# A new order table for the steps of an attention, token-mixer and routed-attention kernel

## The chip, the cores and the metric

The kernel runs on 1 core of a Trainium2 chip. The metric is the device time of one execution in microseconds (us), the median of several runs; lower is better. One core has five engines with an instruction queue each: TensorE (PE in the rows; PEld is its weight load), VectorE (DVE), ScalarE (ACT), GpSimd (POOL) and SyncE (SP), which here only issues transfers between DRAM and the on-chip memory. Each engine takes its own list strictly in order; an instruction that waits for another engine or for a transfer holds everything behind it on its own engine.

## The reference

Three stages, one after the other, for 4 batches of 448 tokens. A first attention has 12 heads of width 64 on normed queries and keys; a mixer works over tokens (448 to 256 and back) and over channels (768 to 1536 and back); a second, causal attention has 4 experts of width 64, of which each token uses two.

```python
def _attn_ref(q, k, v, g_q, g_k):
    q_n, k_n = (rmsnorm(q, g_q), rmsnorm(k, g_k))
    scores = scale * np.matmul(q_n, k_n.transpose(0, 1, 3, 2))
    scores = scores - np.max(scores, axis=-1, keepdims=True)
    attn = np.exp(scores)
    attn = attn / (np.sum(attn, axis=-1, keepdims=True) + 1e-09)
    return np.matmul(attn, v)
def _moe_ref(x, w_tok1, w_tok2, w_ch1, w_ch2):
    h = np.maximum(x.transpose(0, 2, 1) @ w_tok1, 0.0) @ w_tok2
    u = x + h.transpose(0, 2, 1)
    return u + np.maximum(u @ w_ch1, 0.0) @ w_ch2
def _moe2_ref(x, w_gate, wq, wk, wv, wo):
    # two largest gate logits of each token, softmax over these two: w
    for e in range(E):
        q, k, v = x @ wq[e], x @ wk[e], x @ wv[e]
        scores = np.where(causal, -1e9, scale * (q @ k.transpose(0, 2, 1)))
        a = softmax(scores)
        out += w[token, e] * (a @ v @ wo[e])
```

## The kernel before

The whole computation is cut into 3,840 steps. A step is a few instructions on one engine: the scores of one or two chunks of 112 queries (`weighted`, line 712 on PE), the row maxima (line 682 on DVE, written to `nm`), their scaling (line 688, on DVE or POOL), the exponentials (line 697 on ACT, out of the accumulator banks `s` into the tiles `s`), the flips of the weights (PE transposes, line 736, into the banks `a`, each then copied out by `copy` on ACT, line 541, or on DVE, line 542), the product with the values (`attend`, line 835), the transposes of its result (line 861), and the large products with the weights (`product`, line 630). The accumulator banks `s`, `m` and `a` are rings of two buffers: the third user waits until the first has been copied out.

For batch 0 the first attention comes by itself; from then on the side work (the first attention of batch b+1 and the second of batch b-1) stands among the products of `channel(b)`, whose weights are loaded into the ring `whl` of 6 buffers, the first time from the inputs, later from copies in DRAM (`kept_c1`, `kept_c2`, line 621).

For the pairs of heads of batches 1 to 3 `spread` (lines 773 to 799) turns the sums of the exponentials into a row: two small DVE operations on `inv` (lines 782 and 784), a write of the row to DRAM (line 786), and two reads of it, spread over the partitions, into `rn` (line 798). In `normalize` the reciprocal `rc` (line 869) stands ahead of the scaling of the transposed result into `xn` (line 880). In `project` the gate is some 30 small DVE operations (`tiny`).

The order of the steps is not found when the kernel is built. `Plan.issue` reads it from a table, a compressed string in which each step has its place and its engine:

```python
def issue(self):
    ...
    for k in self.read():
        self.steps[k][2](self.by[k])
```

The costs that steps are added with, and their `port` mark (this step and the steps of the other engine with that mark don't run together), are used by `lay` and `order`, a model that lays steps out in time; `issue` calls neither.

Of the kernel before, what the change touches and what calls it, by code (L numbers as in the profile page):

```python
# [21 lines left out]
EPS_SUM = 1e-9  # L22
# [34 lines left out]
    r"c-nPY3w#vSxu5@;nIyXl2_zv2gg3||SV0sE3Mk%dTPjk4i&e3p0yY&yt@MI`dVeVRs#IIAC~rj+sD%pD=jEXwjr9Q{Mo=NVl"  # L57
    r"Mo<4LfB+?=iKkSW@h8Pi@TYfbI$ktfB)~B)nY)(W$<jEF^4sccs~vsx4Nt2cc2cbEM%e{iAYlp>U!Zg-oW$|0OPFf0-S&QZ0"
    r"lPxf0he+vBKoMSR-aU|Jok3-!$hd^u0FIeP{K+_X<w6ImL=9Sph#qyYkTPn2kp<x69OV%w0J9Sr>KL_cQ)%W0t#d*doMFvd;"
    r"Wa!F`KyR0!prjuqkO__}1o!N2eax*pDKyJ5sM9G?@L)2VbOJ2?2>$Dc_3#li2JGMmUux5K6_+%2kzp6HK*rwiKMnd#2%SI$m"  # L60
    r"caiRz(OBb@@<QG>uSr<^rcySr#?#IVuHZWw(1AlHiq+_BnR=@FAXY!U7j&|Q*EOmDBis3u1M(!q9d4p<;vANeL(s6p{k!`z1"
    r"@weL#aOYowv0L4buL92Bn322ed~fH{gBO1o`xZLZ58htf?I2K}o9JFK(A{+4#YcO8da0ZFb!IUe=<c*(7m~E0-@bJJi=~)y{"
    r"fPnRHeOP?_=<yN1KMB8xLx$>&nRYgHAB&f$VYr6B?U+<M{dibli0gB{PUHAzuPgg?YFr&HJPnDoqww9`hLZ408h82!}O1#1t"
    r"@_IeI_zqMaM^m?Xd4&$_L+%O|`k_++?)w&eZe;k<IwUW79`>x#ioh3f+Qne8J;Q5f535rjSFMH;oy(wJ`H&GWOD)8Hr&wFJJ"
    r"mRrravCP4CwxT=~xz{;+JxKM`3taoI<^ZO$LL1@`ear;3~Yo;R(0u-J$p==ptlpKWL@zm0fm%wKQKYmHj=#<*6%x=FRI9vmt"
    r"bYW6-xcXP3xLc5lYMelt>QtNvUboW)Qo7yI|el(#k8+q<Y+ImSDP*p9?pbhe**jZ~aW?c(RJ(9f|wJqV)c0Iek=ojp4YvlGV"
    r"pZ|}gI~T0OXl&+`K;)lRhq_?jCQN9PLxFndCi>_@dEIh=%>0iEH@7U`KACUFxQirq=G((gAcu}@1ai^S-Z8qSoW5Oc@95S#&"
    r";6)3kHq--6ml<kJePl0-S1e>ok9<K?H3l-^lHHlbp>nbZX0tT&T6}V(VyXb6RQ<Q<YiMV_xE7z80*Q|XBcoOUe%vgIs)59xg"
    r"WR5$M*JMefhcV9WF<0xfCm2RfEv_pS_Wvx2$Iy6ktzLS=SRo`8%1MUG<rL9nS9?h_XRga~Y(=`DK(eO8OU7-K$s$@O9BO>#w"
    r"G&-8S0Ymy5R<A41zs7NR3xIg#(}jpxUIIPSUWo7)Wiq_$^)UA4aum#mzM+4GT6Q!UkR9Jz6tjN{o9@;)87+5V9DV>~Ss;3T?"  # L70
    r"UwWfOe-<DqM_Iv+yZp9@v3;q*m36@ir{n>K<^1TZy$c372oIP-H{%oX{aCZMM$F^AXLFM0C;^A4JUq8Xda`%IRYwLIaYeezF"
    r"Q8$0Y?`ic^*--o*6ANmj|3XQ@eN;O~TJZdN*s++c96zgf3;Sp9#U3pk_iov*%AVqjN-L=rVr0_1TONwL(e)EojEC1__A?Lfe"
    r"F5|SZA&~do4;<4i#^ig+^NF4kz4rWWix>3k$42Ky;wsG58({qWWmMX)-Rt#Fi3t_$x(m*np@XC@cM6_Xc3Q!IMij=%~*MHRD"
    r"C@zt7^Mw((<!+FaE_&J8~9Nm;R2HmrQ=?VeiT@XYx_K;E$!(QH(aNaDKB2tLf^tEW{&m&?mB%zPl=Gd>n4-E!5rd)~|2a47M"
    r"t(5rWeikypHdPu~5>RE&D16fc*2^-aYGBzh}`*$W=9J^LB#y$t18at~X~c&aq%3cET3PRgOeKhS#aG=lnvH@tNv(Cy7nr~QR"
    r"3cyN(Tv;g<FOC}TK3nyV{$C8sjX?5<A1~;qz*b8+0ucFKZ-L(4SIb4Mec^EnLUy(O{`84nnro35)dyraF@8YgSrJUJpdHuco"
# [353 lines left out]
def kernel(  # L430
# [20 lines left out]
    S = CP * NCH  # L451
# [966 lines left out]
```

## Time and profile before

| what | us |
|---|---|
| median of 3 runs | 835.11 |
| lowest and highest run | 835.08, 835.37 |
| the profiled execution, its own time | 836.71 |
| span of its instructions | 834.6 |
| TensorE busy in the span | 809.7 |
| VectorE, ScalarE, GpSimd busy | 614.1, 478.8, 128.7 |

The span goes from the first to the last instruction of the profiled execution; the 2.1 us to its own time lie around it. The granted clock of TensorE is at its upper level in nearly all of the span.

### The profile page before, as it was taken

The numbers are of one execution on the slowest core, as the hardware profiler recorded it, in microseconds if no ns is written. First come the engines' busy times: TensorE is split into PE (matmuls) and PEld (weight loads), VectorE is DVE, ScalarE is ACT, GpSimd is POOL, SyncE is SP. The second block draws the span as 40 slices with busy tenths as digits, with TensorE's granted clock in tenths as the row PEclk, the third lists the DMA queues.
The fourth block names the chain that finished last, engine by engine and source line by source line (L and its number), as shares of the span: only waits on it lengthen the run. The fifth ranks groups of instructions, "written<-read, shape, count | busy, mean of one in ns | idle before, by whom it ended". The sixth has DMA issues, their size and how long they took to land.

```text
span 834.6 us, 13125 instructions
## 1 busy us (share of the span) xinstructions
PE 809.7 (97%) x4508; PEld 631.6 (76%) x4508; DVE 614.1 (74%) x1298; ACT 478.8 (57%) x1053; POOL 128.7 (15%) x154
## 2 busy tenths in 40 slices
PE   4999899999999999999999999999999999999998
PEld 1446597878667878778776977767877888999886
DVE  6999999989999896977888688786665665221362
ACT  6898886777889548465466447643653631011243
POOL 3024201121542014130011010101120020000100
PEclk9999999999999999999999999999999999999999
DMA  8658879989876467887647515784666306776444
GB/s 227 179 176 202 261 238 272 303 284 287 277 241 194 146 191 250 236 286 219 207 139 207 204 29 172 237 230 163 207 194 176 126 2 207 211 219 201 150 145 174
DMA packets 83202, 168.37 MB, mean 202 GB/s; under 512 B 17504, under 2 KB 39136, under 8 KB 83136
## 3 DMA queue, kind: packets, MB, share of 16 engines
q1 hardware_dynamic: 82992, 167.54, 65.9%
q8 instruction: 36, 0.59, 0.3%
q14 instruction: 30, 0.25, 0.1%
q10 hardware_dynamic: 144, 0.00, 0.0%
HBM read 136.66 MB, written 30.84 MB: 201 GB/s over the span
## 4 chain that ended last, share of the span: by engine, by line
PE 87%; DMA 4%; DVE 4%; ACT 3%; issue 1%; SPq 0%; ACTq 0%; DVEq 0%
PE a L630 61%; PE s L712 10%; PE m L835 10%; PE m L861 2%; PE s L760 2%; ACT s L697 1%; DMA nat<-in_nat_dram 1%; PE a L736 1%; DMA whl<-kept_c 1%; PE s L736 1%; DMA xhl<-in_nat_dram 1%; DVE nm L682 1%; DMA rn<-inv 1%; ACT s L541 0%; DVE st L938 0%
## 5 line engine op out<-in xcount | busy, mean ns | idle before, releaser
L630 PE MATMUL a<-uhl,whl 128*128 128x448 f32 x1152 | 240.7, 364 | 0.1
L630 PEld LDWEIGHTS a<-uhl,whl 128*128 128x128 f32 x1152 | 213.7, 188 | 24.6 <-issue 6.8
L630 PE MATMUL a<-hid,whl 128*128 128x448 f32 x864 | 180.2, 365 | 1.7 <-DMA whl<-kept_c 1.6
L630 PEld LDWEIGHTS a<-hid,whl 128*128 128x128 f32 x864 | 160.3, 187 | 23.7 <-issue 8.5
L697 ACT ACTIVATE s<-s,nm,st 128x448 f32<-128x448 f32 (+1 forms) x192 | 137.5, 723 | 57.6 <-DVE nm L688 41.1
L822 ACT COPY s<-s 32x896 f32<-32x896 f32 (+1 forms) x134 | 111.1, 829 | 39.6 <-DVE s L810 37.9
L712 PE MATMUL s<-k,q 64*128 64x448 f32 (+4 forms) x512 | 111.3, 549 | 4.8 <-ACT s L697 4.1
L682 DVE TENSOR_REDUCE nm<-s 128x2 f32<-128x896 f32 (+1 forms) x96 | 101.6, 1079 | 11.7 <-PE s L712 11.5
L835 PE MATMUL m<-s,v 128*64 128x448 f32 x384 | 77.5, 545 | 0.7 <-ACT s L822 0.7
L712 PEld LDWEIGHTS s<-k,q 64*112 64x112 f32 (+1 forms) x512 | 41.3, 184 | 48.3 <-issue 26.3
L1219 DVE TENSOR_TENSOR u<-a,u 128x448 f32<-128x448 f32 x48 | 29.8, 621 | 57.6 <-PE a L630 57.5
L810 DVE STREAM_TRANSPOSE s<-s 128x896 f32<-128x896 f32 x60 | 63.5, 1088 | 4.1 <-ACT s L697 2.7
L822 DVE COPY s<-s 32x896 f32<-32x896 f32 (+1 forms) x91 | 59.1, 650 | 2.3
L835 PEld LDWEIGHTS m<-s,v 128*64 128x64 f32 x384 | 25.8, 136 | 43.2 <-issue 39.6
L697 ACT ACTIVATE s<-s,nm 112x448 f32<-112x448 f32 (+3 forms) x64 | 31.0, 493 | 38.0 <-DVE nm L676 37.4
L546 ACT ACTIVATE hid<-a 128x448 fp32r<-128x448 f32 x27 | 14.6, 541 | 66.1 <-PE a L630 65.9
L1208 DVE SCALAR_TENSOR_TENSOR hid<-a,hid 128x448 fp32r<-128x448 f32 x48 | 29.6, 619 | 30.8 <-ACT hid L546 30.3
L560 POOL TENSOR_TENSOR uhl<-u,uhl 128x448 fp32r<-128x448 f32 x23 | 27.7, 1219 | 148.8 <-DVE uhl L542 141.7
L560 POOL TENSOR_TENSOR whl<-wraw,whl 128x384 fp32r<-128x384 f32 (+1 forms) x28 | 29.8, 1067 | 110.4 <-ACT whl L541 43.5
L630 PE MATMUL a<-whl,uhl 128*112 128x260 f32 x288 | 38.6, 287 | 0.0
L697 ACT ACTIVATION_READ_ACCUMULATOR s<-s,nm,st 128x1 f32 (+1 forms) x192 | 38.3, 199 | 0.0
L676 DVE CUSTOM_DVE_ANT_0 s<-s,veil 112x112 f32<-112x112 f32 (+3 forms) x64 | 28.3, 461 | 12.5 <-PE s L712 11.5
(149 smaller groups left out, 1039.3 us busy)
## 6 DMA issues: line engine op xcount, KB each, us to landing
whl<-kept_c SPq DMA_DIRECT2D x144, 384.0 KB, 4.0
w<-in_wc_dram SPq DMA_DIRECT2D x48, 384.0 KB, 3.9
kept_c<-whl SPq DMA_DIRECT2D x48, 384.0 KB, 4.7
whl<-kept_qk SPq DMA_DIRECT2D x24, 384.0 KB, 3.7
nat<-in_nat_dram SPq DMA_DIRECT2D x19, 448.0 KB, 5.2
v<-in_vals_dram SPq DMA_DIRECT2D x24, 256.0 KB, 6.5
q<-in_qkt_dram SPq DMA_DIRECT2D x24, 232.0 KB, 5.6
k<-in_qkt_dram SPq DMA_DIRECT2D x22, 224.0 KB, 4.9
```

The costliest lines, as they stand in the source:

```text
L560: either(n, reads, writes, lambda e: e.tensor_tensor(dst()[:, 1], src(), f(dst()[:, 0]), op=ALU.subtract))
L630: nc.tensor.matmul(acc, lhs[:, x], rhs[:, y], start=first and i == 0, stop=last and i == 2)
L676: dve(w + 40, [], [pst, (nm, (c, j))], lambda e, j=j: e.tensor_tensor_reduce(pst.t[:CP, j, :w], pst.t[:CP, j, :w], veil[:, S - w :], -1.0, ...
L682: lambda e: e.tensor_reduce(nm.t[:R, c], pst.t[:R, :, :w], axis=AX.X, op=ALU.max, negate=True))
L697: lambda j=j: nc.scalar.activation(s.t[:, c, j, :w], pst.t[:R, j, :w], AF.Exp, bias=nm.t[:R, c, j : j + 1], scale=-1.0 if rq is None else ...
L712: nc.tensor.matmul(pst.t[:R, j, :w], q.t[me, CP * c : CP * c + R], k.t[me, :w], start=True, stop=True)
L736: nc.tensor.transpose(ps()[:, i, CP * r : CP * r + CP], s.t[:, r].rearrange("p j k -> p (j k)")[:, P * m : P * m + P], ident[:CP, :CP])
L810: dve(2 * S - 4, [(s, (j, r)) for j in range(2)], [(t, r)], lambda e, r=r: e.transpose(t.t[:, :, 32 * r : 32 * r + 32], s.t[:, r].rearrang ...
L822: lambda e, a=a, o=o, w=w, at=at: (nc.scalar.copy if e == "ACT" else ENG[e].tensor_copy)(at(p.t[32 * o : 32 * o + 32, :, P * a : P * a + N ...
L835: nc.tensor.matmul(av.t[64 * j : 64 * j + 64, q0:S], vat(j, c)[1](), p.t[:, j, c, q0:] if causal else p.t[:, 3 * j + c], start=c == 0, sto ...
L1208: lambda e, hl=hl, pa=pa: e.scalar_tensor_tensor(hl.t[:, 1], pa.t[:, :S], 0.0, f(hl.t[:, 0]), op0=ALU.max, op1=ALU.subtract))
L1219: dve(S, [pa], [u], lambda e, u=u, pa=pa: e.tensor_add(u.t, pa.t[:, :S], u.t))
```

## The change

The table is another one. The same 3,840 steps with the same dependencies are issued in another order, and 381 of them on another engine (of those that can run on two or three): GpSimd has 133 steps instead of 122, VectorE 1,140 instead of 1,153, ScalarE 798 instead of 796, TensorE (1,202) and SyncE (567) as many as before. Of TensorE's steps 797 stand at another place of its list. Two groups of small VectorE steps get the `port` mark, which only the model reads. The longer table moves all later line numbers up by 8: line 736 before is line 744 after.

```diff
 TABLE = (
-    r"c-nPY3w#vSxu5@;nIyXl2_zv2gg3||SV0sE3Mk%dTPjk4i&e3p0yY&yt@MI`dVeVRs#IIAC~rj+sD%pD=jEXwjr9Q{Mo=NVl"
...
         mine = lambda: inv.t[:CP, : 2 * NCH]
         dve(2 * NCH, [p.sm], [inv], lambda e: e.tensor_scalar_add(
-            mine(), p.sm.t[:CP].rearrange("p j c -> p (j c)"), EPS_SUM))
-        dve(80, [], [inv], lambda e: e.reciprocal(mine(), mine()))
+            mine(), p.sm.t[:CP].rearrange("p j c -> p (j c)"), EPS_SUM), port=True)
+        dve(80, [], [inv], lambda e: e.reciprocal(mine(), mine()), port=True)
...
-        tiny = lambda reads, writes, fn: add("DVE", 78, reads, writes, fn)
+        tiny = lambda reads, writes, fn: add("DVE", 78, reads, writes, fn, port=True)
```

**VectorE at the end of the first attention of batch 0.** Before, in front of the scaling of the last result (`xn`, in the trace at 100.5 us); `m_1085` and `m_1136` are the transposed results of two head pairs:

```order
L868 TENSOR_SCALAR rc_1124<-sm_669 112x16
L580 SCALAR_TENSOR_TENSOR wraw_1106<-wraw_1106,w_1000 128x384
L542 CAST whl_1127<-wraw_966 128x384
L582 SCALAR_TENSOR_TENSOR wraw_1106<-w_1000,wraw_1106 128x384
L542 CAST whl_1130<-wraw_966 128x384
L930 SCALAR_TENSOR_TENSOR k_898<-k_898,gqk,rb_991 128x448
L560 TENSOR_TENSOR whl_1130<-wraw_966,whl_1130 128x384
L560 TENSOR_TENSOR uhl_1025<-u_851,uhl_1025 128x448
L560 TENSOR_TENSOR whl_1127<-wraw_966,whl_1127 128x384
L869 RECIPROCAL rc_1124<-rc_1124 112x16
L880 TENSOR_TENSOR xn_1144<-m_1085,rc_1124 112x4x128
```

After, the same place (`m_1116` and `m_1140` are the two transposed results):

```order
L876 TENSOR_SCALAR rc_1084<-sm_676 112x16
L550 CAST whl_1086<-wraw_950 128x384
L877 RECIPROCAL rc_1084<-rc_1084 112x16
L588 SCALAR_TENSOR_TENSOR wraw_1079<-wraw_1079,w_989 128x384
L590 SCALAR_TENSOR_TENSOR wraw_1079<-w_989,wraw_1079 128x384
L550 COPY oT_1121<-m_1088 128x448
L888 TENSOR_TENSOR xn_1127<-m_1116,rc_1084 112x4x128
```

Eight operations on weights and keys stood between the first of the two `rc` operations and the reciprocal; now one stands there, and three between the reciprocal and the scaling.

**ScalarE at the last flips of the first attention of batch 0.** Before, from the squares of a later load (`nat`) to the five copies of flipped weights out of the banks `a` (`s_1017<-a_1036` and on); two more were copied by VectorE:

```order
L990 ACTIVATE nat_979<-nat_979 112x1024
L575 ACTIVATE wraw_966<-w_914 128x384
L578 ACTIVATE w_914<-w_914 128x384
L541 ACTIVATE whl_1021<-wraw_799 128x384
L541 ACTIVATE uhl_1025<-u_851 128x448
L541 ACTIVATE s_1017<-a_1036 128x448
L541 ACTIVATE s_1017<-a_1041 128x448
```

After, the same place (ScalarE copies six of the seven blocks out, the first of them `a_997`):

```order
L998 ACTIVATE nat_958<-nat_958 112x1024
L549 ACTIVATE whl_1018<-wraw_950 128x384
L583 ACTIVATE wraw_950<-w_934 128x384
L549 ACTIVATE s_1004<-a_997 128x448
L549 ACTIVATE s_1004<-a_1030 128x448
L549 ACTIVATE s_1004<-a_1036 128x448
```

Three operations instead of five stand in front of the first copy of a flipped block, and one more copy stands on this engine.

**SyncE's transfers in the channel products of batch 2**, where the fourth batch's first attention runs beside them. Before; `whl143` to `whl147` are weights, `rn_3_10` is the row of one head pair, `rn13` its two reads, `q26`, `q27` and `v21` loads for later pairs:

```order
L621 DMA whl143_5838<-kept_c2_0_3_10_1763 128x768
L1075 DMA rb19_5809<-rs_3_30_5784 64x448
L786 DMA rn_3_10_5843<-inv13_5672 112x2x4
L621 DMA whl144_5929<-kept_c2_0_4_00_1819 128x768
L1075 DMA rb20_5811<-rs_3_30_5784 64x448
L621 DMA whl145_5932<-kept_c2_0_4_10_1839 128x768
L798 DMA rn13_5938<-rn_3_10_5843 64x448
L1061 DMA q26_5940<-in_qkt_dram 128x464
L1061 DMA q27_5942<-in_qkt_dram 128x464
L798 DMA rn13_5938<-rn_3_10_5843 64x448
L621 DMA whl146_5945<-kept_c2_0_5_00_1915 128x768
L1079 DMA v21_5947<-in_vals_dram 128x512
```

After, the same place (`q26` and `q27` stand ten rows further up):

```order
L794 DMA rn_3_10_5860<-inv13_5726 112x2x4
L1087 DMA v20_5876<-in_vals_dram 128x512
L806 DMA rn13_5883<-rn_3_10_5860 64x448
L629 DMA whl143_5889<-kept_c2_0_3_10_1738 128x768
L806 DMA rn13_5883<-rn_3_10_5860 64x448
L629 DMA whl144_5901<-kept_c2_0_4_00_1819 128x768
L629 DMA whl145_5965<-kept_c2_0_4_10_1842 128x768
L629 DMA whl146_5967<-kept_c2_0_5_00_1915 128x768
L629 DMA whl147_5969<-kept_c2_0_5_10_1855 128x768
```

The reads of the row now stand in front of `whl143` and `whl144`, and four weight loads follow each other with nothing between them.

## Rows read from the trace of the kernel before

**Rows 1.** The page: span, and TensorE's busy time, share of the span, instructions.
```profile
span 834.6 us, 13125 instructions
PE 809.7 (97%) x4508; PEld 631.6 (76%) x4508; DVE 614.1 (74%) x1298; ACT 478.8 (57%) x1053; POOL 128.7 (15%) x154
```

**Rows 2.** Busy time by stretch: length, then us (instructions) of each engine, granted clock.
```profile
0.00:25.00 25.00, 11.71 (x32) 4.40 (x33) 17.67 (x42) 16.56 (x33) 6.96 (x19) 1.00 0.76 193
25.00:102.00 77.00, 72.12 (x439) 40.46 (x441) 72.27 (x144) 69.08 (x174) 20.17 (x26) 1.00 0.74 211
102.00:803.00 701.00, 697.74 (x3860) 563.59 (x3861) 510.98 (x1059) 380.69 (x818) 101.57 (x109) 1.00 0.66 202
803.00:835.00 32.00, 28.12 (x182) 23.14 (x181) 13.21 (x56) 12.46 (x30) 0.00 (x0) 0.99 0.55 186
```

**Rows 3.** Timeline of TensorE, its longer waits: start, us, instruction, idle before it.
```profile
53.70 0.98 PE L736 MATMUL a<-ident,s 112*128 112x112 f32 x8 [0.65 <-ACT s L541]
...
91.90 1.04 PE L736 MATMUL a<-ident,s 112*128 112x112 f32 x8 [1.06 <-ACT s L541]
93.14 0.60 PE L736 MATMUL a<-ident,s 112*128 112x112 f32 x4 [0.20 <-ACT s L541]
...
101.33 0.62 PE L861 MATMUL m<-ident,oT 128*112 128x128 f32 x4 [0.97 <-DVE xn L880]
...
236.07 3.23 PE L835 MATMUL m<-s,v 128*64 128x448 f32 x16 [0.69 <-ACT s L822]
...
563.72 4.45 PE L630 MATMUL a<-hid,whl 128*128 128x448 f32 x21 [1.56 <-DMA whl<-kept_c]
```

**Rows 4.** Timeline of VectorE before the wait at 101.33.
```profile
100.15 0.24 DVE L869 RECIPROCAL rc<-rc 112x16 f32<-112x16 f32 x1
...
100.49 0.69 DVE L880 TENSOR_TENSOR xn<-m,rc 112x512 f32<-112x512 f32 x1
```

**Rows 5.** Timeline of ScalarE before the wait at 91.90.
```profile
88.60 1.06 ACT L990 ACTIVATE nat<-nat 112x1024 f32<-112x1024 f32 x1 [0.77 <-DMA nat<-in_nat_dram]
...
90.86 0.56 ACT L541 ACTIVATE uhl<-u 128x448 fp32r<-128x448 f32 x1
91.33 0.95 ACT L541 ACTIVATE s<-a 128x448 f32<-128x448 f32 x2
```

**Rows 6.** Timeline from 545 to 553 us: VectorE, and SyncE's issues of transfers.
```profile
545.65 0.20 DVE L784 RECIPROCAL inv<-inv 112x8 f32<-112x8 f32 x1
...
548.76 0.54 SPq L786 DMA_DIRECT2D rn<-inv  x1
...
550.39 0.54 SPq L621 DMA_DIRECT2D whl<-kept_c  x1
552.96 0.45 SPq L798 DMA_DIRECT2D rn<-rn  x1
```

**Rows 7.** The chain that ended last, same stretch: start, us, what.
```profile
548.76 4.19 DMA rn<-inv
...
555.06 8.52 DMA whl<-kept_c
```

**Rows 8.** The page's DMA issues: count, KB each, us to landing.
```profile
whl<-kept_c SPq DMA_DIRECT2D x144, 384.0 KB, 4.0
```

**Rows 9.** Timeline of the start: GpSimd's first maxima, ScalarE's first exponential.
```profile
12.93 0.20 POOL L688 TENSOR_TENSOR nm<-nm,st 112x2 f32<-112x2 f32 x1 [5.59 <-DVE nm L682]
...
15.11 0.71 ACT L697 ACTIVATE s<-s,nm,st 112x448 f32<-112x448 f32 x1
```

**Rows 10.** GpSimd and VectorE at 239 us, and all of line 782 (ns: least/median/most).
```profile
239.34 2.23 POOL L560 TENSOR_TENSOR uhl<-u,uhl 128x448 fp32r<-128x448 f32 x2
239.40 1.10 DVE L782 TENSOR_SCALAR inv<-sn 112x8 f32<-112x8 f32 x1
...
L782 DVE TENSOR_SCALAR inv<-sn x18: 127/164/1102, 109.2 to 640.9; 112x8 f32<-112x8 f32 x18
```

More of the change, by code (lines that the diff above doesn't have):

```diff
@@ L62 @@
[L62 to L76, printed above, removed]
@@ new lines @@
+    r"3V9dpyE6td2i2d+g_feMwt}vh}X|sdpVMWvOOq=c}dOCP!BPyr*dWlzGD!pV{-)W68|NQWm<$r=EE7tNBw)@B87NtBYXRra<"
+    r"kCrek;ST}&pwRU7$EFu&K3+_WVVGXe6KPR#7nY2>y6i<^&|_#$hhn=dvQcYWA;l3^4y-Ix8&eBT^8D|K@6l<5ofMN`L~$XS("
+    r"grD93l^0A+mFp~Q8y35T<YO;pD>mB&bSJ@c_J<bjrndQ}s+|h@!(hmN0Z@0oL_nO7y3J%<u_}<tL2JO5r^VUund?+(>^FJc|"
+    r"J0IQbDS?ceP}1+$gq8<M=fho2Rk#>|M1UqsTJ<~92^{+#{3thi?RZ~sVYbHygY?8Lm6`O?9Y#q^Fuv)IW><2*Zh6~($3-|k`"
+    r"lrCC31ddV(0f15d2CF4c8?!jKX$xT-t1ylm!qfjgEJey-7WR&zmw$ReZAnziZMJ$WJB4|-#R9bTwQYT{Ir|oOEw^u8arYhF!"
@@ new lines @@
+    r"omGetj#(S&?vH7BSWhUwz>Dv&p3_;okJE&Ok2k7vVle1I#rJJod@-PP-hz^;<t4dTFww#e$vi!Q&qdGD>@NGU94-yTQG^gZ^"
+    r"j;II9o)-~4q&dbb}2SIqo%`q}N@g0mK!)8?g@nmwMLx$3P?8h1a)6;~}zo&eBc!l3%3fHSJaYklha<gDE@bK<C0;Q0!i5M1}"
+    r"{U(V(ncYgb_aAV)!ysg^L9@?turkmpS_|WhFYVIHAFfO+6wf22J_&?*#oK=540Z=x~ySC??W!wLGpzPF;Vt|qnk1Y2k7Zr71"
+    r"*E9a7y)VaH^!#|AXFuFil~{hNwEw~TNX!SxZ+-q__k_ed$g2RQt<UW`_iEQ`O{+^=7}c?QMeb^@<er3ITf|i*9_qY%$+uNmA"
+    r"9e3_ym;`*_TK_z`zjar>w2-Q>>sq<ynm3NxMzK?Bpw`oYJ2ydCleF@2hgVVX}vgj=|MQyJ*b=KyRqFMQr;X=>WMF*;-{bc^D"
@@ new lines @@
+    r"R|Bx9}vL_nc{Qrgb$yVQV-$bYs`@#Ok0k`j@1Zre4{!!k1JEdh_j&+*0443@uumB<yTPTq5{LaeCl#Vz%y!*AvU3xZ>`vUnH"
+    r"4Tah?lh#UfCUsGE91t3z2o-b=2;B*$L?XnH8MD7Eyi1BLf{O#Sc!6>zbz<%M7b>zA}XB`*0=%c9id-M+dzmYmBmzq~tX&*Px"
+    r")2k`#f7rsbsntkB9@r19U2p_b(IAO^JZ+7b0bKO20`0?4hTD8f`-8T4a5<q=Q{3k=-Z`ZH*{hr(&fj_R_SCm&h8P?1^<1O|1"
+    r")05A2UiM6M>hO8X`m_OK*`pCfu=|bDB@-(6>Gw=H|N4gbLtS23S$qZ7O@))K<F7V5y>nCyoiQxFP2(d;Pc2Q@SG{M!^m(lYu"
+    r"Xtg!3$n?i|0HJio7Bov{QP`KI=3)-^XZfQJ8sQ->eKJ@h9yn<pu^HTUwo?svZl|N6;r(aWcx}Hmx<F>uc@4}K%cfK=$O1%ht"
@@ new lines @@
+    r"AEtOA04^R?>J>NzLyCr&~Y7^1j;hVc+1cTM#|G;NJZ`e(7}Wy|M4@&xspVIquGcQL|^iPoA&)Oq={jn)kU?ua2KKwrg$iig$"
+    r"BkV-`HssN_`&QBadGvmkxC-u`m%%e)ofnl<07pTib8JN;4o$OcFpV5YoXGqNVHa?TB-@s<6BPm@iUu=+^-*)`*9KP*ltaZPd"
+    r";Bu3P3sATsYjTnA?=bati-?I1Jt#cpjlKVLcI0rxFURzIZWRB^{9t9WpBm4l(dTit>ShL=x2_JL9%V2{a{5sD82RnAia&A64"
+    r"H)5j`>Rk^ydTmQw+81)VZJQrF0;KO3=E$NQODFC<Id1Q9m}D-2Pk$b{=FLfOX_MQYdA8@%k6+e*&=>AYCD3x}b1g3<_c?6PG"
+    r"dZ8Y5PBM5)xyirDv(I3)-US`>z?I&v8K`yoWkBb{g?93M~_+BB$vGG1xIj{>6i=c^QkfFJw2gf-$(C%H{`RP&#jG~b6z(e|6"
@@ new lines @@
+    r">m2Mjh+Q>H?~IG`S`_ps-}^6YUvCHQ9!(DM5xCh(aH3x17;+sYenXVnf-L3gq;J-ibg++9uWnp~)s9`B>7b{I#mUDtRJ%98r"
+    r"q#N3#k;%_^#UOJD6WQiHlitm09GVpkniMkul_)()|{q+L!Zu80`*VAzPHS8CO#{6b*!hMGNaBo|&H{X<w#b)peF@5J^A8B3f"
+    r"(rV4Sd#&bf$<s=a)ylQfCmIE4SBy@gUS3H9=1&$6Hwh>LuhALeotPJoWej)|ws;U4QbS6ZC%qgZH>pdhvLfmCVOeK~oBuhwy"
+    r"16*Oj?(@WorlkzCX+5DKq$ny>5ytOlc5V~_QboPir8T$N5e0=88uG|COA)ZTYS5b1dZ`}PD`aceY@}Kf3;Imt*At5caqz(WX"
+    r"gG(f8J1Y1jFQtVMr%0!sCG<bVM>Z65+JhitBlBr3^dZ<g>69+6{x%+Yh(W87=d@P)B!JLBd{96{{dgYAt("
```

115 lines of the change are left out of this document (57 added, 58 removed).

## The prediction

> **What bounds the kernel now.** I read the page first. TensorE is busy in 809.7 of 834.6 us [rows 1]; no other engine comes near, so what can be won is TensorE's idle time, 24.9 us, as long as its own work is the same. It is: the change removes and adds no matmul, and the 4,508 of them stay. Where products, scores, flips and value products follow each other, a block's first matmul costs a little more; the number of such changes in TensorE's list goes from 266 to 260, which I take as nothing.
>
> Then the busy time by stretch, which says where the 24.9 us lie [rows 2]: 25.00 - 11.71 = 13.3 us up to 25 us (loads arrive and the first scores run through their chain once), 77.00 - 72.12 = 4.9 us from 25 to 102 us (the rest of batch 0's first attention), 701.00 - 697.74 = 3.3 us in the long middle, and 834.6 - 803 - 28.12 = 3.5 us at the end, of which nearly all is the last copy and the last store. Beside TensorE, VectorE is busy in 72.27 and ScalarE in 69.08 of the 77 us of the second stretch: three engines nearly full, handing small pieces to each other. In the middle VectorE and ScalarE have 190 and 320 us to spare.
>
> Last the waits one by one [rows 3]. In the second stretch they are short and nearly all end with a copy out of a bank by ScalarE or VectorE: 0.65 at 53.70, 1.06 and 0.20 around 92, 0.97 at 101.33. In the middle there are few: 0.69 at 236.07, and 1.56 at 563.72, where weights came late. What an order table can reach is these two stretches, 4.9 + 3.3 = 8.2 us; start and end hang on transfers and on one chain of operations each.
>
> **The change part by part.** The `port` marks alone do nothing: `issue` reads the table and calls no model. The table is everything, and I cost it at the places that I can read in both orders.
>
> At 101.33 TensorE waited 0.97 us for a scaling that started at 100.49, right behind the reciprocal at 100.15 [rows 3, 4]. Eight operations had been put in front of that reciprocal; in the new list one stands there and three behind it, one of them the copy that TensorE's next transposes need. I take the whole 0.97 as won.
>
> Around 92 TensorE waited 1.06 + 0.20 us, because ScalarE did five operations from 88.60 on before its first copy of a flipped block at 91.33 [rows 3, 5]. Now three stand there, so the first copy comes about 1.8 instead of 2.7 us after the squares begin (two short ones go, at the 0.47 from 90.86 to 91.33 each); but ScalarE copies six of seven blocks instead of five, at 0.95 / 2 = 0.48 us each, and the banks are still emptied by mostly one engine. A gain of 0.9 and a loss of 0.5 where 1.26 was lost: between nothing and all of it I take half, 0.6.
>
> At 53.70 (0.65) the new list has two blocks of transposes instead of one between the flips that wait and those before. Such a block covers some 0.6 us (the one at 101.33 took 0.62 [rows 3]); but ScalarE's copy of the last block now stands behind two more exponentials. Again half: 0.35. The stretch's other waits, 4.9 - 0.97 - 1.26 - 0.65 = 2.0 us, I leave as they are.
>
> At 563.72 (1.56) the chain is a transfer of weights that took 8.52 us from its issue [rows 7] where 4.0 is the median [rows 8]. In front of it SyncE's queue had stood still: the row written at 548.76 had landed only 4.19 us later, and the read of it held the queue from 550.93 to 552.96 [rows 6, 7]. Then two loads of queries, two reads and the weights went out together and shared the DMA engines. In the new list the queries are issued earlier and four weight loads stand together behind the reads. I take the whole 1.56 as won.
>
> On the other side: at the start a transfer and a small VectorE operation now stand ahead of things that count, and the squares of one head pair come later. The cover is that the first maxima are scaled at 12.93 + 0.20 while their exponentials start only at 15.11, behind other work of ScalarE [rows 9]: 2.0 us, which should hold it; 0 to 0.5, taken as 0.2. And 797 of 1,202 places on TensorE's list are new, so there will be waits that weren't there. The nearest thing to a price is the middle stretch, where a wait is 0.7 to 1.6 us [rows 3]; I take one of 1.0, between none and three.
>
> Sum: - 0.97 - 0.6 - 0.35 - 1.56 + 0.2 + 1.0 = - 2.3 us. The profiled execution took 836.71 us (834.6 of span and 2.1 around it), 1.6 above the median of the runs; the span would be 832.3, and the median 835.11 - 2.3 = 832.8. The bounds: all reachable idle time gone, -8.2; none of it and three new waits of 1.6, +4.8 and the 0.5 of the start.
>
> More of the small work goes to GpSimd: 133 steps instead of 122, among them ten more copies of line 822 and seven more splits of `uhl`. One row shows what that can cost VectorE: at 239.40 an operation with 8 elements per partition took 1.10 us, where half of its kind take under 0.164, while GpSimd ran two splits [rows 10]. That is 0.94 us per hit; eleven hits are 10 us of VectorE, against 190 us of its idle time in the middle, so the sum takes it as nothing. The Trainium skill (GPSIMD Engine Reference, sections 1 and 8) says that the two engines share their interfaces to the on-chip memory, and that GpSimd contends with VectorE instructions that have two inputs there or use a two-port mode. By that rule every added GpSimd step is a risk to VectorE, which speaks against this change; the row at 239.40 is of the kind that the rule describes, and it carries the third rival below.
>
> **The rivals.** First, the waits come back elsewhere. In the second stretch VectorE (72.27) and ScalarE (69.08) have 5 and 8 us left of 77 [rows 2], and the new table moves work between them without making it less: a copy that is early here makes an exponential late there. Then only the wait for weights is won, and the new wait takes most of it: 835.11 - 1.56 + 1.0 = 834.6, no change. For it: three full engines. Against it: the waits at 92 and 101 come from a poor place in a list, not from too much work.
>
> Second, the wait for weights gets longer. The new list has only one issue (`v20`) between the row's write and its first read, and `whl143` with all later weights stands behind that read. The row takes 4.19 us to land [rows 7]; less 0.8 for the two issues the queue is held for 3.4 us instead of 2.0, so the wait at 563.72 would be 1.56 + 1.4 = 3.0 instead of nothing: 832.8 + 3.0 = 835.8. It decides as soon as the weights in stock (four halves) are used up before the hold and a landing of 4.0 us [rows 8] are over. Against it: the reciprocal that starts all this came 3.1 us before the row's write [rows 6], and if it is early now, the hold falls where the stock is full.
>
> Third, and on the other side, GpSimd holds VectorE up where TensorE waits for it. A hit costs 0.94 us [rows 10], and where the instruction hit, or the one behind it, empties a bank, TensorE waits for as much. The gains of 2.3 are used up by the third hit on such a copy, and from the fifth on the kernel is slower than the bound: 832.8 + 5 x 0.94 = 837.5. Against it: in the middle stretch TensorE hardly waits for VectorE at all (the waits shown end with ScalarE or a transfer [rows 3]).
>
> **How the numbers follow.** A measurement of this kernel can tell about 0.2% (1.7 us) from no change: faster is below 833.4, slower above 836.8. The forecast, 832.8, gets 0.45 (its own range 829.5 to 833.4); the first rival 0.30 (833.4 to 836); the second 0.10, of which three quarters lie within 0.2%; the third 0.15. So faster 0.45, same 0.37, slower 0.18. The range, 830.0 to 837.0, leaves out about 0.08 below, where most of the reachable waits are gone, and 0.1 above, where five or more copies are hit or the start is late as well.
>
> **What would show it.** TensorE's busy time unchanged to within 1 us. Idle time from 25 to 102 us down from 4.9 to about 3, with no wait of a microsecond at the last flips and none at the last transposes of batch 0. No wait for `kept_c` weights in the channel products of batch 2, and the row's write further in front of the weights' issue. Up to 25 us the same 13.3, give or take 0.5. If the second stretch keeps 4.9 us, the first rival holds; a wait of some 3 us for `whl` shows the second; VectorE's small operations of 0.9 us and more beside GpSimd's splits, with TensorE waiting for VectorE, the third. A new wait of several microseconds in the middle, or a start that is later by more than 0.5, would make the forecast wrong in a way that I have not priced.

## The result, and the profile after

The changed kernel takes 842.09 us (median of 4 runs, 840.99 to 842.29) against 835.10 of the kernel before on the same chip (4 runs): ratio 1.0075, 95% interval 1.0047 to 1.0103. It is slower by 0.75%, 7.0 us, and lies outside the predicted range.

The page of the new kernel, span and busy times (line numbers are 8 higher than before):

```profile
span 840.2 us, 13127 instructions
PE 810.6 (96%) x4508; PEld 631.9 (75%) x4508; DVE 610.7 (73%) x1285; ACT 480.0 (57%) x1055; POOL 149.2 (18%) x170
```

TensorE's busy time is 0.9 us longer than in [rows 1]. The granted clock of this one run was lower at the start (0.86 and 0.96 in the first two rows below, 1.00 in [rows 2]): from 18 to 31 us it was 0.50, the lower of its two levels, after 18 us in which TensorE had been busy for 6.2. That need not be the reason for the 0.9 us, since opening_new and early, further down, have 810.5 and 812.3 us at a granted clock of 1.000; nor is it the loss, since a run of the new kernel at 1.000 throughout took 842.15 us. GpSimd has 20.5 us more. The idle time of TensorE is 840.2 - 810.6 = 29.6 us instead of 24.9. These two, 5.6 us, are the difference of the two profiled spans. The busy time by stretch, columns as in [rows 2]:

```profile
0.00:25.00 25.00, 10.61 (x31) 3.90 (x31) 17.65 (x43) 16.20 (x32) 7.12 (x20) 0.86 0.81 215
25.00:102.00 77.00, 72.25 (x424) 39.61 (x425) 72.38 (x133) 70.47 (x175) 22.97 (x26) 0.96 0.66 189
102.00:803.00 701.00, 693.90 (x3829) 560.31 (x3828) 501.95 (x1036) 381.09 (x819) 119.09 (x124) 1.00 0.67 203
803.00:841.00 38.00, 33.83 (x229) 28.04 (x227) 18.74 (x76) 12.22 (x33) 0.00 (x0) 0.99 0.49 168
```

Up to 25 us TensorE is idle for 14.4 us (13.3 before), from 25 to 102 us for 4.75 (4.88), in the middle for 7.10 (3.26), at the end for 840.2 - 803 - 33.83 = 3.4 (3.5). So the second stretch neither won nor lost, and the middle lost 3.8 us. (The edge at 25 us cuts through a wait. Up to 28 us the idle time is 14.6 us instead of 13.3.) The longer waits of TensorE in its timeline, which answer to [rows 3]:

```profile
10.69 1.84 PE L720 MATMUL s<-k,q 64*112 64x448 f32 x4 [1.32 <-DMA q<-in_qkt_dram]
...
25.25 1.20 PE L744 MATMUL a<-ident,s 112*128 112x112 f32 x5 [1.01 <-ACT s L705]
...
65.45 0.99 PE L744 MATMUL a<-ident,s 112*128 112x112 f32 x8 [1.30 <-DVE s L550]
...
82.33 0.98 PE L744 MATMUL a<-ident,s 112*128 112x112 f32 x8 [1.07 <-DVE u L1198]
...
230.16 1.87 PE L638 MATMUL a<-hid,whl 128*128 128x448 f32 x8 [1.25 <-DVE whl L568]
...
272.92 3.23 PE L843 MATMUL m<-s,v 128*64 128x448 f32 x16 [0.57 <-DVE s L830]
...
278.58 0.62 PE L869 MATMUL m<-ident,oT 128*112 128x128 f32 x4 [1.19 <-DVE oT L862]
...
352.52 8.68 PE L638 MATMUL a<-hid,whl 128*128 128x448 f32 x42 [1.64 <-DVE hid L1216]
...
386.78 3.23 PE L843 MATMUL m<-s,v 128*64 128x448 f32 x16 [0.48 <-DVE oT L862]
...
512.28 1.49 PE L638 MATMUL a<-xhl,w 128*128 128x448 f32 x6 [0.72 <-DVE ot L550]
```

All four places of [rows 3] that the prediction counted as won are gone: no wait at the flips around 53 and 92 us, none at the last transposes of batch 0, none for weights in the products of batch 2. In their place stand waits that end with VectorE: 1.30 and 1.07 in the first attention, then 1.25, 0.57, 1.19, 1.64, 0.48 and 0.72 in the middle, where before no long wait ended with VectorE. The last is not wholly new: the old kernel waited 0.52 for ScalarE at the same place (509.30).

Why VectorE is late shows when its timeline is laid beside GpSimd's. VectorE ahead of six of these waits:

```profile
61.29 2.35 DVE L876 TENSOR_SCALAR rc<-sm 112x16 f32<-112x16 f32 x1
...
64.84 0.56 DVE L550 COPY s<-a 128x448 f32<-128x448 f32 x1
...
80.37 1.30 DVE L588 SCALAR_TENSOR_TENSOR wraw<-wraw,w 128x384 uint32<-128x384 uint32 x1
...
226.85 1.22 DVE L550 CAST whl<-wraw 128x384 fp32r<-128x384 f32 x1
228.00 1.28 DVE L588 SCALAR_TENSOR_TENSOR wraw<-wraw,w 128x384 uint32<-128x384 uint32 x1
...
348.19 1.67 DVE L696 TENSOR_TENSOR nm<-nm,st 128x4 f32<-128x4 f32 x1
349.89 1.92 DVE L830 COPY s<-s 32x896 f32<-32x896 f32 x2
351.84 0.62 DVE L1216 SCALAR_TENSOR_TENSOR hid<-a,hid 128x448 fp32r<-128x448 f32 x1
...
383.21 2.29 DVE L938 SCALAR_TENSOR_TENSOR k<-k,gqk,rb 128x448 f32<-128x448 f32 x1
...
509.64 0.97 DVE L696 TENSOR_TENSOR nm<-nm,st 128x4 f32<-128x4 f32 x1
```

GpSimd at the same times:

```profile
59.88 3.73 POOL L568 TENSOR_TENSOR xhl<-xn,xhl 112x1024 fp32r<-112x1024 f32 x1 [5.17 <-DVE nm L696]
...
80.24 1.01 POOL L568 TENSOR_TENSOR whl<-wraw,whl 128x384 fp32r<-128x384 f32 x1
...
226.71 1.15 POOL L568 TENSOR_TENSOR uhl<-u,uhl 128x448 fp32r<-128x448 f32 x1
227.92 1.78 POOL L830 COPY s<-s 32x896 f32<-32x896 f32 x2
...
347.95 1.89 POOL L999 TENSOR_TENSOR nat<-nat 112x1024 f32<-112x1024 f32 x1
349.82 1.45 POOL L940 TENSOR_SCALAR k<-k,gqk 128x448 f32<-128x448 f32 x1
...
383.13 1.89 POOL L999 TENSOR_TENSOR nat<-nat 112x1024 f32<-112x1024 f32 x1
...
507.22 3.37 POOL L568 TENSOR_TENSOR uhl<-u,uhl 128x448 fp32r<-128x448 f32 x3 [1.41 <-DVE uhl L550]
```

And what two of these VectorE operations usually take in this trace (ns: least/median/most):

```profile
L696 DVE TENSOR_TENSOR nm<-nm,st x42: 121/163/1665, 24.1 to 603.2; 128x4 f32<-128x4 f32 x22, 112x2 f32<-112x2 f32 x14, 112x4 f32<-112x4 f32 x6
...
L876 DVE TENSOR_SCALAR rc<-sm x7: 165/168/2345, 45.0 to 814.1; 112x16 f32<-112x16 f32 x7
```

The reader is to see the ends. VectorE's `nm`, four elements per partition, ends at 348.19 + 1.67 = 349.86, GpSimd's squares at 347.95 + 1.89 = 349.84; `rc` ends at 63.64, the split at 63.61; the `nm` at 509.64 ends at 510.61, the last of three splits at 510.59. The small operation doesn't run slowly, it stands until GpSimd's instruction is over. Of the eleven VectorE operations with at most 16 elements per partition that took 0.2 us or more beyond the median of their kind in this trace, ten end 0.01 to 0.03 us behind a GpSimd instruction. Behind `nm` stand two copies and then `hid`, for which TensorE waits 1.64 us.

### The profile page after: what moved, and what is told of

It is laid out like the page before. It is cut to its first block, busy times and chain, and to the rows that moved or that the text cites. A ratio compares the mean times of both kernels' runs of the same rounds, so it can differ in the third digit from the quotient of the medians.

```text
span 840.2 us, 13127 instructions
## 1 busy us (share of the span) xinstructions
PE 810.6 (96%) x4508; PEld 631.9 (75%) x4508; DVE 610.7 (73%) x1285; ACT 480.0 (57%) x1055; POOL 149.2 (18%) x170
## 4 chain that ended last, share of the span: by engine, by line
PE 80%; DVE 11%; DMA 4%; ACT 2%; issue 2%; SPq 1%; DVEq 0%; ACTq 0%
PE a L638 57%; PE s L720 9%; PE m L843 8%; DVE nm L690 2%; PE m L869 2%; PE s L768 2%; DVE s L818 2%; DMA rn<-rn 1%; PE s L744 1%; PE a L744 1%; ACT s L705 1%; DVE s L830 1%; DMA nat<-in_nat_dram 1%; DVE st L946 1%; DMA w<-in_wc_dram 1%
## 5 line engine op out<-in xcount | busy, mean ns | idle before, releaser
L690 DVE TENSOR_REDUCE nm<-s 128x2 f32<-128x896 f32 (+1 forms) x96 | 101.7, 1082 | 14.9 <-PE s L720 14.4
L568 POOL TENSOR_TENSOR uhl<-u,uhl 128x448 fp32r<-128x448 f32 x30 | 35.9, 1205 | 218.6 <-ACT uhl L549 102.6
L830 DVE COPY s<-s 32x896 f32<-32x896 f32 (+1 forms) x79 | 54.4, 689 | 2.1
L705 ACT ACTIVATE s<-s,nm 112x112 f32<-112x112 f32 (+3 forms) x64 | 31.1, 491 | 34.5 <-DVE nm L684 33.8
L1216 DVE SCALAR_TENSOR_TENSOR hid<-a,hid 128x448 fp32r<-128x448 f32 x48 | 29.6, 619 | 21.6 <-ACT hid L554 20.8
L568 POOL TENSOR_TENSOR whl<-wraw,whl 128x384 fp32r<-128x384 f32 (+1 forms) x24 | 25.2, 1059 | 86.0 <-DMA kept_c<-whl 30.5
L638 PE MATMUL a<-xhl,t 112*128 112x256 f32 x288 | 37.3, 282 | 0.3 <-ACT s L549 0.2
```

The costliest lines, as they stand in the source:

```text
L568: either(n, reads, writes, lambda e: e.tensor_tensor(dst()[:, 1], src(), f(dst()[:, 0]), op=ALU.subtract))
L638: nc.tensor.matmul(acc, lhs[:, x], rhs[:, y], start=first and i == 0, stop=last and i == 2)
L690: lambda e: e.tensor_reduce(nm.t[:R, c], pst.t[:R, :, :w], axis=AX.X, op=ALU.max, negate=True))
L705: lambda j=j: nc.scalar.activation(s.t[:, c, j, :w], pst.t[:R, j, :w], AF.Exp, bias=nm.t[:R, c, j : j + 1], scale=-1.0 if rq is None else ...
L830: lambda e, a=a, o=o, w=w, at=at: (nc.scalar.copy if e == "ACT" else ENG[e].tensor_copy)(at(p.t[32 * o : 32 * o + 32, :, P * a : P * a + N ...
L1216: lambda e, hl=hl, pa=pa: e.scalar_tensor_tensor(hl.t[:, 1], pa.t[:, :S], 0.0, f(hl.t[:, 0]), op0=ALU.max, op1=ALU.subtract))
```

## The experiments

Each group ran on one chip with the kernel before beside it (836.7 to 838.1 us there, single runs 834 to 840), so only ratios to it are compared. The new kernel itself wasn't run again in these groups: its 1.0075 is that of the result above. All kernels but `gp_short` differ from the new one in the table alone. In the diffs, `old` and `new` are the two tables, `[:n]` is a table up to TensorE's n-th step and `[n:]` the rest; a step is named by the tile that it writes and its time in the profile.

### Which part of the list loses

```diff
-table = new
+table = new[:131] + old[131:]     # opening_new
+table = old[:131] + new[131:]     # rest_new
```

> Stitched list: the new table's order and engines up to the end of batch 0's first attention (the first 131 of TensorE's 1,202 steps, some 103 us; these are the same steps in both tables), then the old table's order and engines to the end. If the loss is where TensorE's idle time is in the two profiles, only the start is later here (14.4 us of idle time instead of 13.3 up to 25 us) and 25 to 102 us is the same (4.75 against 4.88): 835.1 + 1.1 - 0.1 = 836.1. If most of the loss came from the opening (its order upsets what follows), 840 or more. If the late start is only the profiled run's, 835.

> The other half: the old table up to some 103 us, the new one from there. By the idle time of the two profiles (7.10 us instead of 3.26 in the middle): 835.1 + 3.8 = 838.9, and up to 841 if the old kernel's profiled run, which was 1.6 us above its median, had its wait for weights at 563.72 of 1.56 us only there. If the opening is to blame: 835 to 836.

Measured: opening_new 1.0018 (1.0005 to 1.0032), rest_new 1.0063 (1.0038 to 1.0087). The two add up to the whole: 0.18 + 0.63 = 0.81% against 0.75%. The waits came back at their places in both (1.31 and 1.08 in the one, 1.24, 1.64, 0.49 and 0.72 in the other), so they belong to the lists and not to a run.

### Is it the engines of the 381 steps?

```diff
-engine = new.engine
+engine = old.engine               # engines_back: all 381 steps
+engine[25 copies of line 830, 4 squares of nat: POOL] = ACT     # gp_relief
```

> The new table's order of all steps, but every step on the engine that the old table gives it (381 steps go back). If the loss hangs on where small work runs (GpSimd's splits, squares and copies beside VectorE's instructions): the new waits at 230, 352 and 387 us shrink or go, and the time is 835 to 838. If the order itself is to blame: 840 to 843. A rival of its own: an order made for other engines puts copies late everywhere, and the time is above 845; then this kernel says nothing of either.

> The new table, with the 29 GpSimd steps that ScalarE can do (25 copies of line 830, four squarings of nat) done by ScalarE, at the same places of the order. If GpSimd's neighbourhood makes VectorE late where TensorE waits: the waits at 352.52 (1.64) and 386.78 (0.48) go, which lie right behind GpSimd's squares, and half of the 1.25 at 230.16, which lies behind copies and a split: 842.1 - 1.64 - 0.48 - 0.6 = 839.4. If the order is to blame, they stay: 842. If ScalarE's own work is now late: above 843.

Measured: engines_back 1.0422 (1.0391 to 1.0453), which is the rival of its own: list and engines belong together, and the run decides nothing. gp_relief 1.0100 (1.0076 to 1.0124), no faster than the new kernel; of the three cases of its forecast it is the last, ScalarE late. Its profile says why: the waits at 230, 352 and 387 us are gone, as the theory of GpSimd said, but ScalarE with 29 more steps is late elsewhere: 1.87 at 238.89, 1.21 at 363.52 and 0.69 at 534.26, all ending with ScalarE. The cause could not be read from the time; smaller changes had to follow.

### GpSimd beside VectorE, in the middle

```diff
-                    else nc.gpsimd.tensor_mul(qv(), qv(), qv()))
+                    else nc.gpsimd.tensor_mul(*[qv()[..., :2]] * 3))
-        nc.gpsimd.tensor_scalar_mul(k, k, gqk)
-        nc.gpsimd.tensor_tensor(k, k, r, op=ALU.mult)
+        nc.gpsimd.tensor_scalar_mul(k[:, :32], k[:, :32], gqk)
+        nc.gpsimd.tensor_tensor(k[:, :32], k[:, :32], r[:, :32], op=ALU.mult)
-            nc.vector.tensor_reduce(dst, src, axis=AX.X, op=ALU.add)
+            nc.vector.tensor_reduce(dst, src, axis=AX.X, op=ALU.max)
-        for k in range(5, -1, -1):     # adding up on GpSimd
+        for k in (0,):
```

That is gp_short. The other kernel leaves nothing out:

```diff
+engine[squares of nat at 347.95 and 383.13] = ACT               # sq_act
```

> The new table unchanged, but GpSimd's operations that work in place (the squares of nat, the scaling of k, the adding up of nat) cover only a few of their columns, so each takes some 0.2 us instead of 1.4 to 3.4; VectorE's adding up takes the maximum instead of the sum at the same length, so that nothing negative comes under the root. The output isn't the reference's. No other engine gets any work for it. If GpSimd's long operations hold VectorE up: VectorE's nm at 348 us takes 0.2 instead of 1.67, its k at 383 us 0.7 instead of 2.29, and TensorE's waits at 352.52 (1.64) and 386.78 (0.48) go, perhaps the 0.72 at 512.28 and part of the 1.07 at 82.33 too: 842.1 - 2.1 = 840.0, down to 838.8. If the copies are late by their place in VectorE's list: all waits stay, 842.1.

> The new table, with two steps on another engine: the squares of nat beside the waits at 352.52 and 386.78 are done by ScalarE at their places in the order. All work is done. By the theory of GpSimd's neighbourhood the two waits go (1.64 + 0.48), and ScalarE pays 0.95 us twice where it is busy in 65 of 100 us: 840.0, or 841 if one exponential is late in their place. By the theory of the order: 842.1.

Measured: gp_short 1.0030 (1.0016 to 1.0044), sq_act 1.0033 (1.0017 to 1.0049). Both lose the waits at 352.52 and 386.78 entirely. VectorE in sq_act, with the same list as in the new kernel:

```profile
348.62 0.42 DVE L696 TENSOR_TENSOR nm<-nm,st 128x4 f32<-128x4 f32 x1
349.07 1.50 DVE L830 COPY s<-s 32x896 f32<-32x896 f32 x2
350.60 0.62 DVE L1216 SCALAR_TENSOR_TENSOR hid<-a,hid 128x448 fp32r<-128x448 f32 x1
...
381.96 0.68 DVE L938 SCALAR_TENSOR_TENSOR k<-k,gqk,rb 128x448 f32<-128x448 f32 x1
```

`nm` takes 0.42 instead of 1.67, `k` 0.68 instead of 2.29. Two of 3,840 steps on another engine win 0.42% (1.0075 to 1.0033, two chips) where the two waits would be 0.25%; the idle time from 102 to 803 us falls from 7.10 to 701 - 696.62 = 4.38, which is 0.32%. Against early, below, which ran beside it and keeps the two waits, sq_act wins 0.29%. The 0.72 at 510 us stays in both kernels, and so does the 1.07 at 82 us in gp_short, of which the forecast had hoped to win a part. Neither lies beside the in-place work: the rows above show a split of `uhl` beside the `nm` at 509.64 and a split of `whl` beside the `wraw` at 80.37, and these kernels leave both splits on GpSimd. No run took them away.

### The late start and the late row

```diff
 SyncE, start
+load of q0
 load of w31 (second piece of the token weights)
-load of xhl, first half
-load of q0
+load of xhl, first half
 VectorE and SyncE, 260 us: reciprocal of inv5 and write of its row
-reciprocal 15 rows of the table behind the first step on inv5, write behind the reads of rn4
+reciprocal right behind the first step on inv5, write ahead of the second read of rn3
```

> The new table with four rows moved and nothing else: the first load of queries goes out one row earlier (before the second piece of the token weights, as in the old table), and the reciprocal of the sums of the last head pair of batch 1 and the write of its row stand as early as their inputs allow. If the late start hangs on that load (TensorE waited 1.32 for it at 10.69, and at 230 to 280 us 0.57 and 1.19 behind VectorE, which waited 1.74 for the spread row): 842.1 - 0.5 to 1.3 - 1.2 to 1.8 = 839.0 to 840.4. If the start is late by the DMA engines' load as a whole, its 1.1 us stay: 840.5. If VectorE is late there for its own work and not for the row: 841 to 842.

Measured: 1.0062 (1.0041 to 1.0084), unclear against the new kernel's 1.0075. The start didn't come earlier: up to 28 us TensorE was idle for 15.0 us, against 14.3 in opening_new, which has the load at the new table's place, 14.6 in the new kernel and 13.3 in the old one. TensorE now waited 1.16 and 1.52 for two blocks of keys at 10.94 and 14.30. The late start isn't that one load. The waits of 0.57 and 1.19 around 275 us were gone in this run, but others stood where the order is the new kernel's: 1.74 at 154.59, behind a VectorE that had waited 2.23 for ScalarE, and 0.57 for weights at 572.68. In mended, below, they were not (0.61 and 0.94) although the row was written at 263.64 instead of 265.56: there the read of the row was issued at 271.04, when VectorE had just ended the scaling at 270.79 that still used the buffer. In early that read stood behind the scaling too (273.52 and 273.27), so this doesn't tell the two runs apart. I don't count these waits as settled.

### Are the predicted gains real?

```diff
-table = old
+table = old[:633] + new[633:]     # late_new
+table = old[:685] + new[685:]     # won_late
+old, ACT: s_552<-a_582 ahead of the exponential in front of it;     # won_open
+     whl_1021 and uhl_1025 behind four copies of flipped blocks; the copy of oT ahead of the squares
+old, DVE: RECIPROCAL rc_1124 behind TENSOR_SCALAR rc_1124; xn_1144 ahead of three splits
```

> The old table up to the first 633 of TensorE's steps (some 460 us; the same steps in both tables), the new one from there. The prediction's term of 1.56 us for the weights at 563.72 should be won without any of the new waits of the first 460 us: 835.1 - 1.56 + 0.2 (the wait at 512.28 is 0.72 instead of 0.52 there) = 833.7, faster than the old kernel by 0.16%. If the weights are late with any order, or the wait was chance of one run: 835.1.

> The old table with seven rows moved and nothing else, at the three waits that the prediction counted in the second stretch: at 53.70 a copy of a flipped block goes ahead of one exponential; at 91.90 four copies go ahead of two copies of splits (the split on GpSimd that needs one of them moves along); at 101.33 the reciprocal and the scaling go ahead of seven and three VectorE rows, and the copy of the last result out of its bank ahead of ScalarE's squares, since a look at ScalarE shows that this copy ended at 100.9, so that the earlier scaling alone would win only some 0.3. If these waits come from poor places in a list, as the prediction said: 835.1 - 0.55 - 1.06 - 0.97 = 832.5. If the second stretch is full and they come back elsewhere: 835.

> The old table up to TensorE's step 685 (some 490 us), the new one from there; the seam lies where only four other steps differ (the seam at step 633 made a wait of its own of 4.0 us behind a spread row that was loaded late). Without the wait for weights at 563.72 or 564.95 (1.56 and 1.06 in two profiles): 833.5 to 834.1. If weights are late with the new order too: 835.1.

> Both of the two before: 831.0 to 832.5 if each gain stands by itself, and so faster than the old kernel by 0.3 to 0.5%.

Measured: late_new 1.0051 (1.0034 to 1.0069), a miss that comes from its seam: TensorE waited 4.01 at 482.04 for `h`, whose VectorE step stood behind a `k` that waited 5.97 for a row read which SyncE had issued only at 476.28. With the other seam won_late is at 0.9984 (0.9970 to 0.9999), as forecast, and there is no wait for weights near 564 us. The interval only just leaves 1 out, but the profiles bear it out: from 515 to 790 us TensorE is idle for 1.56 us in the old kernel and 0.87 to 1.28 in three others with the old order there, and for 0.00 to 0.08 in ten with the new order on the new engines (the other two of these: early 0.66, gp_relief 1.72 with its late ScalarE). won_open 0.9996 (0.9983 to 1.0009) is its forecast's second case; won_both 0.9989 (0.9974 to 1.0003) falls short of its forecast. TensorE in won_open at the places of the three waits:

```profile
91.81 1.04 PE L744 MATMUL a<-ident,s 112*128 112x112 f32 x8 [0.34 <-ACT s L549]
...
100.30 0.62 PE L869 MATMUL m<-ident,oT 128*112 128x128 f32 x4
...
103.74 1.61 PE L638 MATMUL a<-t,h 128*128 128x448 f32 x6 [0.59 <-DVE h L1180]
```

1.06 became 0.34, 0.97 nothing, and at 103.74 there is a new 0.59 behind VectorE; others of 0.56 (159.37) and 0.75 (685.61) stand in this profile further on. The waits were poor places in a list, but winning them was worth nothing that could be measured (0.17% at most by the interval).

### Adding the repairs up

```diff
+table = old[:131] + new[131:], squares as in sq_act, row as in early     # mended
+also engine[uhl at 226.71] = DVE, engine[copies at 227.92] = ACT         # mended2
+table = new[:131] + old[131:], engine[xhl at 59.88] = DVE                # open_split
+table = new[:131] + old[131:685] + new[685:], xhl as in open_split       # three_parts
```

> The old table up to 103 us and the new one from there, with two repairs: the squares of nat beside 352.52 and 386.78 on ScalarE, and the row of the last head pair of batch 1 written as early as its inputs allow. Kernel rest_new was at 1.0063 of the old one. If its loss is the sum of its named waits, it gets back 1.64 + 0.49 + 0.59 (squares) and 0.57 (row): 1.0063 - 0.0039 = 1.0024, or 837.1 at 835.1; left are 1.24 at 228.65, 0.64 at 236.70 and 0.72 at 510.17, against the old 0.69 and 1.56. If something is at work that the waits don't show: above 839.

> Kernel opening_new (the new table up to some 103 us, the old one from there) with one step on another engine: the split of xhl that runs on GpSimd at 59.88 us in the new kernel's profile (3.73) is done by VectorE. Beside it VectorE's rc, 16 elements per partition, took 2.35 us, and TensorE then waited 1.30 at 65.45. If GpSimd holds VectorE up there: VectorE gains some 2.2 and pays 1.13 for the split, the wait goes or falls under 0.4: opening_new's 1.0018 - 0.0013 = 1.0005. If the wait comes from the place of the copy in VectorE's list: VectorE has 1.13 more to do, the wait grows to 2 or more: 1.003.

> Kernel mended with three more steps off GpSimd: the split of uhl that ran at 226.71 us goes to VectorE (0.55), the two copies of line 830 at 227.92 to ScalarE (0.9 each). If GpSimd makes VectorE's weights late for the wait at 230.16 (1.25; VectorE's cast took 1.22 there, its wraw 1.28, its split 0.91, where 0.35, 0.55 and 0.55 are usual): the wait goes, 1.0022 - 0.0015 = 1.0007; ScalarE's two copies may make the next product with values late by up to 1.9 us (as in gp_relief at 238.89): 1.0030. If the weights are late by the order: the wait stays at 1.2 or grows by the split, 1.0022 to 1.003.

> The parts of both tables that were worth something: the new one up to 103 us with its split of xhl on VectorE (open_split, 0.9990), the old one from there to TensorE's step 685, the new one after that (won_late, 0.9984). If the two gains are in different waits, as the profiles say, they add up: 0.9974, 832.9 at 835.1. If a gain in the first attention is given back by what follows, as in won_open: 0.9984.

Measured: mended 1.0022 (1.0008 to 1.0036), as forecast, though the gain is the squares' alone. mended2 1.0017 (1.0000 to 1.0033): the wait at 230 is gone, and 0.7 of its 1.25 came back at 238.19 (1.38 instead of 0.65), so that the time says little. The three steps moved at once, so it isn't told apart which of them freed VectorE. VectorE there:

```profile
227.65 0.35 DVE L550 CAST whl<-wraw 128x384 fp32r<-128x384 f32 x1
227.92 0.55 DVE L588 SCALAR_TENSOR_TENSOR wraw<-wraw,w 128x384 uint32<-128x384 uint32 x1
```

0.35 and 0.55 instead of 1.22 and 1.28. open_split is at 0.9990 (0.9979 to 1.0001), against opening_new's 1.0018. VectorE in it:

```profile
61.85 0.17 DVE L876 TENSOR_SCALAR rc<-sm 112x16 f32<-112x16 f32 x1
...
63.05 1.22 DVE L568 TENSOR_TENSOR xhl<-xn,xhl 112x1024 fp32r<-112x1024 f32 x1
...
64.35 0.56 DVE L550 COPY s<-a 128x448 f32<-128x448 f32 x1
```

VectorE did the split itself in 1.22 us, and still came from `rc` to the copy that TensorE needs in 64.35 - 61.85 = 2.50 us, instead of 64.84 - 61.29 = 3.55 in the new kernel, where GpSimd did the split. The wait at 65.45 is gone. three_parts, made of what was worth something, is at 0.9984 (0.9971 to 0.9997): faster than both kernels, but no faster than won_late. Its interval holds the forecast sum, 0.9974, as well, so whether the two gains add up can't be told.

## Why the prediction was wrong

The prediction was 2.3 us faster; the kernel is 7.0 slower.

**The waits won.** The terms of - 0.97, - 0.6 and - 0.35 were right about their places: the three waits are gone in the new kernel. But the stretch has 4.75 us of idle time instead of 4.88, because 1.30 and 1.07 stand at 65.45 and 82.33. That is the first rival for this stretch. For the first of the two open_split shows the cause, GpSimd's split beside VectorE. For the second it can only be read from the rows: the `wraw` at 80.37, two instructions ahead of the `u` that TensorE waits for, took 1.30 instead of 0.55 until GpSimd's split at 80.24 was over; that is 0.75 of the 1.07. won_open adds that even the old list, freed of the three waits, is not measurably faster. In one detail the working was wrong: at 101.33 the copy of `oT` on ScalarE ended only at 100.9, so the scaling alone would not have won 0.97.

**The weights at 563.72.** - 1.56 was right: won_late wins 0.16%, 1.3 us, and most profiles with the new order have no idle time there.

**The start.** + 0.2 (0 to 0.5) was too small. TensorE was idle 1.1 us longer up to 25 us and 1.3 us up to 28, and opening_new lost 0.18% (0.4 to 2.7 us) with a second stretch that gave nothing back. The cover of 2.0 us was read at the first exponential, and the lateness shows at a later one. In the old kernel the flips waited this long for it:

```profile
24.83 1.20 PE L736 MATMUL a<-ident,s 112*128 112x112 f32 x5 [0.57 <-ACT s L697]
```

With the new opening that wait is 1.01 in two profiles and 1.56 to 2.00 in six others. ScalarE's exponential had itself waited for VectorE's `nm`, 1.43 us in the new kernel instead of 0.79. Why `nm` comes late stays open; it isn't the place of the first query load alone.

**The step that failed** is the last positive term with the sentence about GpSimd: "I take one of 1.0, between none and three", and eleven hits on VectorE "against 190 us of its idle time in the middle, so the sum takes it as nothing". In the middle there are five new waits of 0.48 to 1.64 us and one that grew from 0.52 to 0.72, and the part behind 103 us costs 0.63%, 5.3 us, with the gain of 1.56 already in it. VectorE's idle time over 700 us is no cover: an instruction held up is late for what waits on it there, and VectorE's list had no gap between it and the copy that TensorE needed. sq_act and gp_short show it: with the two squares moved, or cut short and given to no other engine, the two waits behind them are gone. In open_split and mended2 the waits of 1.30 and 1.25 go with the GpSimd work beside them. For the 0.72 at 510 us the cause is read from the rows only: the `nm` at 509.64, 0.97 instead of 0.16 us long.

**The third rival** had the mechanism: GpSimd holds VectorE up where TensorE waits for it. Its price of 0.94 per hit was too low for the dearest: these took 1.67 - 0.16 = 1.5, 2.29 - 0.68 = 1.6 and 2.35 - 0.17 = 2.2 us more than usual, since the price is what is left of GpSimd's instruction when VectorE's begins (349.84 - 348.19 = 1.65, 385.02 - 383.21 = 1.81 and 63.61 - 61.29 = 2.32 us), and not a constant. The hits at 226.85 and 228.00 cost 0.87 and 0.73. Its counter-argument, that TensorE hardly waits for VectorE in the middle, was read from the old list, and the change was a new one. By the rule of the Trainium skill (GPSIMD Engine Reference, sections 1 and 8) the VectorE instructions with two inputs in the on-chip memory or in a two-port mode are the ones at risk. The trace agrees: hit were `nm`, `k`, `wraw`, the cast and the copies; `u<-a,u` and `hid<-a,hid`, which read an accumulator bank, kept their 0.6 us beside GpSimd's work.

**The second rival** did not occur in the new kernel's profile; the 0.57 us for weights in early are the nearest thing to it.

**What stays open:** the waits around 275 us and the start are not settled, and for the 0.72 at 510 and the 1.07 at 82 no run shows the cause. The two profiled spans differ by 5.6 of the 7.0 us; the old kernel's profiled run was 1.6 us above its median.

## What to carry to other kernels

Work that is put on GpSimd is not priced by its own engine's idle time, nor by VectorE's: look at which VectorE instruction will run beside it and who waits for the next few behind that. A long GpSimd instruction that no one waits for can be dearer than the same work on a fuller engine, as the split in open_split and the squares in sq_act were. When an order is replaced as a whole, waits that are read off the old list say what can be won there at most; the new list has to be read for new ones. And a wait that is won need not shorten the kernel: in won_open three were gone or cut to a third, and others came up further on.

## What was unexpected of the hardware

A VectorE instruction of four elements per partition stood 1.67 us, until GpSimd's instruction beside it was over, and one of sixteen 2.35. It seems to go both ways, though one case is no proof: GpSimd's split of `xhl` took 3.73 us at 59.88, where VectorE's two-input operations (`wraw`) ran until 61.4, and the next one in the same trace took 2.40.

The first 25 us differ from run to run of the same list: the scores at 16 to 17 us waited 1.54 us for their exponentials in rest_new, 2.99 in won_open and 3.72 in won_late, all with the old opening. Differences of a microsecond at the start should not be read from one profile.
